# A fused SSD scan and maxout layer: the first four up groups in column halves, and another order of the opening steps

## The chip, the cores and the metric

The kernel runs on one core of one Trainium2 chip. The metric is the time of one execution on the device in microseconds (us), as the median of several runs; lower is better. Five engines work side by side, each through its own instructions in a fixed order: TensorE (PE in the profile; PEld is its loading of weights), VectorE (DVE), ScalarE (ACT), GpSimd (POOL) and SyncE (SP), which issues nearly all transfers. They wait for each other on semaphores.

## The reference, cut to what matters

Two stages follow each other. The first is a state-space scan (Mamba 2) over 4 sequences of 768 tokens with 8 heads; the second is a feed-forward layer whose hidden value is the largest of three products.

```python
# x (4, 8, 768, 32), a (4, 8, 768), B and C (4, 8, 768, 16); chunk c of 32 tokens, state (N x D) per head
cum = np.cumsum(log_a[chunk]);  L = exp(cum[i] - cum[j]) for i >= j, else 0
y[chunk] = ((C @ B.T) * L) @ x + (C @ state) * exp(cum)
state = exp(cum[-1]) * state + sum_j B[j] x[j] * exp(cum[-1] - cum[j])
# then, with y as (3072, 256), w1, w2, w3 (256, 768), w_out (768, 256)
h = np.maximum(np.maximum(y @ w1, y @ w2), y @ w3)
out = h @ w_out
```

## The kernel before, in words

**Blocks.** The kernel scans in blocks of 128 tokens of all four sequences, six blocks in all, so a block gives 512 rows (columns of yT) to the feed-forward layer. It uses max(a, b, c) = b + max(a - b, c - b, 0): the weights w1 and w3 have w2 subtracted, and the part of w2 goes straight to the output through the product w2 @ w_out, the "fold". From block one on both layers' products are done with seven quarter products in place of eight (a Strassen form), which needs sums of weights and of activations beforehand. Block zero does its up products plainly, 512 columns at a time.

**Order.** The tile framework adds the waits, and the program's order is the order of each engine's instructions. For the opening, that is for blocks zero to two of the scan with the up layers of blocks zero and one, this order is written by hand: named steps, and a string ORDER that lists them. Behind it a plan in words (STEADY and LAST) does blocks three to five. The names that matter here, with c for a block, b for a sequence and k or n for a number:

- Loads on SP: `f3` to `f11` fetch a block of weights each (512 KB; 3 to 8 are up weights, 9 to 11 are w_out), `cs` stores the running sums of log a, `lLcb` brings them back spread over 128 rows for sequences b and b+1 (1 MB), `lEc`, `lBc`, `lCc`, `lxc` load the rest, `l3` all of block three.
- Decoding the weights (L193 to L222): `dAk` or `dBk` on ScalarE (two instructions, L200 and L202; in dB the value lies in PSUM), `dVk` on VectorE (three: L208, L211, L213), `dPk` the sum on GpSimd (L220).
- Weights made ready: `vk` subtracts w2 (L693, VectorE), `uk` makes the four sums (L703 to L706, GpSimd); `Tq` and `tq` transpose w2 and copy it, `Fq` multiplies it into the fold, `Fc` copies the fold.
- Scan of block zero: `i`, `j` spread the decays in PSUM (PE), `Xbg` their exponentials (ScalarE, L386), `k02`, `k03` masks for two sequences (GpSimd, L390); `tB`, `tC`, `pB`, `bB`, `pC`, `c00`, `c01` bring B and C into place; `s00`, `s02` the scores (PE, L550) and `w0br` their products with L (VectorE, L558; r is a pair of heads). For two of the pairs `q2`, `q3` copy the scores aside (ScalarE) and `M2`, `M3` multiply on GpSimd (L1034). `y00`, `y02` are the two halves of y, two sequences each (PE, L599), and `Y00`, `Y02` copy them into the halves of yT (ScalarE, L609).
- Up layer of block zero: `Gn` is one group of 512 columns in two matmuls (PE, L658), `Hn` its largest value (ScalarE L1131 for w1, VectorE L1133 for w3). Groups 0, 1 need v0; 2, 3 v1; 4, 5 v2; 6, 7 v3; 8, 9 v4; 10, 11 v5.
- Scan of blocks one and two: `kcb` masks (GpSimd, L429), `xci` four exponentials each (ScalarE, L436), `scb`, `wcbr` as above, `Ec`, `dc`, `oc` the part of the old state, `ycb` the own part of one sequence (PE, L586), `Yc0`, `Yc1` copies (ScalarE, L618), `Sci` sums of halves (VectorE, L633). `Dc`, `Ac`, `Zc`, `z1` carry the state on; `fa`, `fb`, `n`, `N` turn the decays over.
- Up layer of block one: `ek` the first four of seven products (PE, L718), `eak` a copy (ScalarE), `evk` sums (VectorE, L756 to L758), `Kk` the other three products, `Kok`, `Kmk`, `Kpk` what follows (Kp on GpSimd, L846). `Oj` and `Oc` are the down layer of block zero (L961), `Sw`, `So` sums of w_out (GpSimd).

**Buffers.** PSUM has eight banks: four for the scan ("att"), one "ffn", one "sumA", two "sumB"; until block one's layer begins the last three serve the opening too. A step that takes a bank waits for that bank's last reader.

Of the kernel before, what the change touches and what calls it, by code (L numbers as in the profile page):

```python
# [19 lines left out]
def kernel(  # L20
# [24 lines left out]
    P = 128  # L45
# [8 lines left out]
    KD = DM // P  # L54
    NF = DF // P
    BLK = NB * P
# [3 lines left out]
    HB = BLK // 2  # L60
# [18 lines left out]
    def bank(tag, n, shape, name):  # L79
        return ps.tile(shape, FP32, tag=tag, bufs=n, name=name)  # L80
# [10 lines left out]
    def ffn_bank(shape, name):  # L91
        turn["ffn"] += 1
        if shared["ffn"] and turn["ffn"] % 3:
            return bank("sumB", 2, shape, name)
        return bank("ffn", 1, shape, name)
# [4 lines left out]
    for k in range(REP):  # L100
# [5 lines left out]
        out=a_sb,  # L106
# [52 lines left out]
    w_sb = [const.tile([P, KD, DF], FP32, name="w%d" % i) for i in range(3)]  # L159
# [74 lines left out]
    def turn_rows(j, name):  # L234
# [24 lines left out]
        out=mask, in_=mask, pattern=[[1, P]], compare_op=ALU.is_ge, fill=MASKED,  # L259
# [3 lines left out]
        out=pick, in_=ident.rearrange("p (r k) -> p k r", k=BH), op=ALU.add, axis=AX.X)  # L263
    npick = const.tile([P, BH], FP32, name="npick")
    nc.vector.tensor_scalar(
        out=npick, in0=pick, scalar1=-1.0, scalar2=None, op0=ALU.mult)
# [4 lines left out]
        out=hsel, in_=hsel, pattern=[[-N, NH]], compare_op=ALU.is_ge, fill=0.0,  # L271
        base=0, channel_multiplier=1)
    nc.gpsimd.affine_select(
        out=hsel, in_=hsel, pattern=[[N, NH]], compare_op=ALU.is_ge, fill=0.0,
# [3 lines left out]
        out=parity, in_=hsel.rearrange("p (r g) -> p g r", g=2), op=ALU.add, axis=AX.X)  # L278
# [163 lines left out]
    yT = {}  # L442
# [203 lines left out]
    def group(bank, i, f, halves):  # L646

        for r in halves:
            for k in range(KD):
                nc.tensor.matmul(  # L650
                    out=bank[:, r * HB:(r + 1) * HB],
                    lhsT=w_sb[i][:, k, f * P:(f + 1) * P],
                    rhs=yT[0][:, k, r * HB:(r + 1) * HB],
                    start=(k == 0), stop=(k == KD - 1), skip_group_check=True)

    def whole_group(bank, i, f):
        for k in range(KD):
            nc.tensor.matmul(  # L658
                out=bank, lhsT=w_sb[i][:, k, f * P:(f + 1) * P], rhs=yT[0][:, k],
                start=(k == 0), stop=(k == KD - 1))  # L660

# [5 lines left out]
    DIFF = (0, 2)  # L669
# [318 lines left out]
    def step(name, fn, *args):  # L988
        assert name not in steps, name
        steps[name] = lambda: fn(*args)  # L990
# [124 lines left out]

    ups = {}

    def up_products(n):
        q, j = divmod(n, 4)
        i, g = divmod(j, 2)  # L1120
        ups[n] = ffn_bank([P, BLK], "up")
        whole_group(ups[n], DIFF[i], 2 * q + g)

    def up_out(n):
        q, j = divmod(n, 4)
# [8 lines left out]
                out=h_of(0)[:, 2 * q + g], in0=mg, in1=ups[n], op=ALU.max)  # L1134

    for n in range(4 * NQ):
        step("G%d" % n, up_products, n)
        step("H%d" % n, up_out, n)
    step("U", places)
    for k in range(NW):  # L1140
# [61 lines left out]
    for j in range(4 * NB):  # L1202
# [4 lines left out]
    step("So", sums_of_out, "G")  # L1207

    ORDER = """
        i0 lB1 tB j0 pB0 X01 f3 X11 tC pC0 f4 f5 X00 X10 bB0 c00 c01 i2 dA0 cs f6 dV0 lL10 f7 f8 lC1  # L1210
        dP0 s00 w002 f9 lE1 lL12 f10 j2 X21 dA1 X20 X30 k02 n2 w003 dV1 w000 X31 s02 q2 dP1 dB2 N2
        w001 k03 M2 dV2 w020 q3 M3 y00 dP2 dB3 Y00 w021 T0 v0 t0 y02 Y02 dB4 G0 H0 dV3 dP3 v1 G1 dV4
        G2 dB5 dV5 fa n1 dP4 v2 G3 G4 N1 dP5 fb H1 D0 dB6 dB7 dV6 H2 dP6 T1 t1 H4 H3 v3 lx1 pB1 bB1
        dV7 dB8 dV8 k10 k11 G5 G6 H5 dP7 A0 dP8 x10 pC1 n3 v4 x11 x12 lB2 H6 U G7 G8 v5 k12 H7 E1 d1
        x13 f11 c10 c11 k13 N3 H8 G9 H9 s10 dB9 u1 Z0 lC2 T2 t2 w100 x14 dV9 dP9 lL20 dB10 w101 x15
        w102 w103 lE2 G10 G11 x16 dV10 dP10 x17 s12 lL22 F0 w120 H10 w122 lx2 w121 H11 o1 y10 D1 y11
        w123 y12 y13 pB2 Y10 u3 Y11 S10 S11 S12 bB2 S13 F1 u0 alone A1 e0 dB11 dV11 Z1 dP11 u2 ea0
        ev0 K0 Ko0 z1 pC2 e1 D2 E2 F2 ea1 ev1 K1 l3 k21 O0 c20 c21 u5 Ko1 d2 e2 ea2 Km1 k22 Fc O1
        ev2 O2 k20 x20 u4 K2 Ko2 O3 s20 O4 x21 x22 x23 Kp1 O5 O6 e3 w203 k23 ea3 ev3 O7 w201 K3 Oc0
        x24 O8 k30 w200 Ko3 Km3 e4 k31 ea4 ev4 x25 O9 O10 s22 w202 w220 x26 w221 Sw So x27 w223 K4  # L1220
        A2 Ko4 Kp3 o2 x30 x31 e5 ea5 y21 Z2 k32 w222 y23 x32 O11 O12 ev5 y20 K5 Ko5 y22 Y20 O13 Y21
        x33 S20 S21 S22 x34 S23 O14 O15 Oc1 k33
    """

    for word in ORDER.split():
# [120 lines left out]
```

## Time and profile before

| what | value |
|---|---|
| median of 3 runs | 261.57 us (261.48 to 265.43) |
| the profiled execution's own time | 261.05 us |
| its span, first to last instruction | 259.3 us |
| PE busy | 247.7 us (96%) |
| PEld busy | 203.1 us (78%) |
| DVE busy | 173.7 us (67%) |
| ACT busy | 115.0 us (44%) |
| POOL busy | 112.9 us (44%) |
| mean granted clock of TensorE | 0.993 |

The page gives the busy time of each engine, a row of 40 slices of the span (a digit is the busy share in tenths), the granted clock of TensorE in the same slices, and the chain of work that ended last, followed back from the end. The timeline lists one engine's instructions in order of time: start, length, line, operation, tile, shape and count, and in brackets the idle time ahead with what ended it. PE's matmuls are pipelined, and one matmul in float32 is two entries.

### The profile page before, as it was taken

To read this page: it belongs to the slowest core of one execution; us is meant where nothing else is said; L and a number is where in the kernel's file an instruction comes from. 1 tells how busy PE (TensorE), PEld (TensorE's weight loads), DVE (VectorE), ACT (ScalarE), POOL (GpSimd) and SP (SyncE) were. 2 spreads that over 40 slices of the span, in tenths; PEclk is the share of its full clock that TensorE was granted. 3 is DMA by queue.
4 is the path that set the end of the run, shared out by engine and by line. 5 is a ranking of instruction groups with operands and counts; after the bars stand their busy time and mean duration, and the time that the engine had idled before them with its cause. 6 is when DMAs were issued, how large, how long until landed. Compare 5 with 4: busy or idle time off the path is not lost.

```text
span 259.3 us, 5617 instructions
## 1 busy us (share of the span) xinstructions
PE 247.7 (96%) x2145; PEld 203.1 (78%) x2145; DVE 173.7 (67%) x360; ACT 115.0 (44%) x310; POOL 112.9 (44%) x148
## 2 busy tenths in 40 slices
PE   6868999899999999999999999999999999999995
PEld 4435454386888778988899988898889899999994
DVE  5599995977626744777765598566878656645651
ACT  3686889933383846634265525163440211101010
POOL 2078683685999940634072651271240404034000
PEclk9988999999999999999999999999999999999999
DMA  3998969996997620966802945501001001001003
GB/s 106 239 228 286 292 143 260 154 216 159 197 252 125 102 52 1 226 169 83 134 4 53 281 108 97 73 5 40 3 1 40 3 0 43 0 0 43 1 19 105
DMA packets 85371, 28.16 MB, mean 109 GB/s; under 512 B 55392, under 2 KB 82016, under 8 KB 85344
## 3 DMA queue, kind: packets, MB, share of 16 engines
q1 hardware_dynamic: 84752, 27.40, 48.1%
q8 instruction: 17, 0.28, 0.5%
q10 hardware_dynamic: 592, 0.39, 0.5%
q14 instruction: 10, 0.08, 0.1%
HBM read 24.54 MB, written 3.24 MB: 107 GB/s over the span
## 4 chain that ended last, share of the span: by engine, by line
PE 87%; DVE 8%; ACT 2%; issue 1%; DMA 1%; POOL 1%; ACTq 0%; DVEq 0%; POOLq 0%
PE o L887 24%; PE sumB L718 20%; PE sumA L718 15%; PE up L658 7%; PE o L961 6%; PE s L550 4%; PE y L586 4%; DVE L L558 2%; PE y L573 2%; DVE w_u L213 2%; PE fold L823 1%; DVE u L211 1%; DVE u L208 1%; PE spread L368 1%; PE A L513 1%; PE trB L464 1%
## 5 line engine op out<-in xcount | busy, mean ns | idle before, releaser
L436 ACT ACTIVATE L<-L,ncums 128x128 f32<-128x128 f32 x160 | 49.7, 391 | 3.7 <-POOL L L429 3.7
L846 POOL TENSOR_TENSOR rb<-h 128x256 f32<-128x256 f32 x16 | 11.7, 729 | 64.0 <-DVE h L793 63.4
L746 ACT COPY eu<-sumA 128x256 f32<-128x256 f32 x30 | 11.2, 372 | 59.4 <-PE sumA L718 59.4
L718 PE MATMUL sumA<-yT,w 128*128 128x256 f32 x120 | 36.9, 389 | 0.1
L718 PE MATMUL sumB<-yT,rb 128*128 128x256 f32 x120 | 35.9, 381 | 0.4 <-POOL rb L703 0.4
L558 DVE TENSOR_TENSOR L<-s,L 128x512 f32<-128x512 f32 x46 | 29.7, 681 | 7.3 <-PE s L550 4.9
L718 PEld LDWEIGHTS sumB<-yT,rb 128*128 128x128 f32 x120 | 22.6, 190 | 4.1 <-POOL rb L703 0.8
L756 DVE TENSOR_TENSOR eu<-sumA,eu 128x256 f32<-128x256 f32 x30 | 12.7, 423 | 18.2 <-ACT eu L746 18.2
L429 POOL TENSOR_SCALAR_AFFINE_SELECT L<-L 128x1024 f32<-128x1024 f32 x20 | 22.6, 1154 | 4.5 <-DMA L<-cums 4.5
L718 PEld LDWEIGHTS sumA<-yT,w 128*128 128x128 f32 x120 | 19.4, 191 | 4.2 <-DVE rb L780 1.0
L658 PE MATMUL up<-yT,w 128*128 128x512 f32 x48 | 21.7, 597 | 0.7 <-ACT yT L609 0.7
L846 POOL TENSOR_TENSOR w<-h 128x256 f32<-128x256 f32 x12 | 8.7, 729 | 28.0 <-DVE h L793 27.5
L220 POOL TENSOR_TENSOR w<-w_u,w_r 128x512 uint32<-128x512 uint32 x9 | 12.8, 1427 | 15.8 <-DVE w_u L213 13.3
L887 PE MATMUL o<-wo,h 128*128 128x128 f32 x120 | 18.0, 275 | 0.0
L887 PE MATMUL o<-rb,h 128*128 128x128 f32 x120 | 18.0, 275 | 0.0
L718 PE MATMUL sumB<-ys,rb 128*128 128x256 f32 x60 | 17.8, 379 | 0.0
L718 PE MATMUL sumB<-ys,w 128*128 128x256 f32 x60 | 17.8, 379 | 0.0
L718 PE MATMUL sumA<-ys,rb 128*128 128x256 f32 x60 | 17.8, 379 | 0.0
L550 PE MATMUL s<-CT,BT 32*128 32x256 f32 x192 | 15.4, 403 | 1.6 <-ACT L L386 1.1
L658 PEld LDWEIGHTS up<-yT,w 128*128 128x128 f32 x48 | 8.7, 190 | 10.1 <-issue 8.6
L780 DVE TENSOR_TENSOR m<-sumB,eu 128x512 f32<-128x512 f32 x15 | 10.3, 688 | 9.0 <-PE sumB L718 9.0
L887 PEld LDWEIGHTS o<-rb,h 128*128 128x128 f32 x120 | 15.7, 192 | 0.0
(149 smaller groups left out, 518.5 us busy)
## 6 DMA issues: line engine op xcount, KB each, us to landing
L<-cums SPq DMA_DIRECT2D x10, 1024.0 KB, 9.1
rb<-in_moe_w_dram SPq DMA_DIRECT2D x9, 512.0 KB, 6.5
raw_x<-in_x_dram SPq DMA_DIRECT2D x6, 512.0 KB, 6.6
out_dram<-ob SPq DMA_DIRECT2D x10, 256.0 KB, 3.1
rb<-in_moe_w_out_dram SPq DMA_DIRECT2D x3, 512.0 KB, 7.2
E<-cums SPq DMA_DIRECT2D x40, 32.0 KB, 4.0
raw_B<-in_B_dram SPq DMA_DIRECT2D x4, 256.0 KB, 5.8
raw_C<-in_C_dram SPq DMA_DIRECT2D x24, 32.0 KB, 1.9
```

Source lines behind the costliest of these rows:

```text
L220: nc.gpsimd.tensor_tensor(out=dst.bitcast(U32), in0=v.rearrange("p (k f) -> p k f", k=2), in1=r.rearrange("p (k f) -> p k f", k=2), op=ALU ...
L429: nc.gpsimd.affine_select(out=Ls[c][:, b], in_=Ls[c][:, b], pattern=[[0, NH], [1, P]], compare_op=ALU.is_ge, fill=MASKED, base=0, channel_ ...
L436: nc.scalar.activation(L[:, b, h], L[:, b, h], AF.Exp, bias=ncum[c][:, b * NH + h:b * NH + h + 1], scale=1.0)
L550: nc.tensor.matmul(out=s[:, i].rearrange("j g i -> j (g i)"), lhsT=st["BT"][rows, b], rhs=st["CT"][rows, b].rearrange("p g i -> p (g i)"), ...
L558: nc.vector.tensor_tensor(out=M, in0=s, in1=M, op=ALU.mult)
L658: nc.tensor.matmul(out=bank, lhsT=w_sb[i][:, k, f * P:(f + 1) * P], rhs=yT[0][:, k], start=(k == 0), stop=(k == KD - 1))
L718: nc.tensor.matmul(out=bank[:, half], lhsT=left(p, k), rhs=sides[c][p], start=(first and half == 0), stop=True, skip_group_check=True)
L746: nc.scalar.copy(out=eu[:, 0], in_=units[c, k][0][:, 0])
L756: nc.vector.tensor_tensor(out=eu[:, 1], in0=A[:, 1], in1=eu[:, 0], op=ALU.add)
L846: eng.tensor_tensor(out=to, in0=a1, in1=a0, op=ALU.subtract)
L887: nc.tensor.matmul(out=o[SLOT[p]], lhsT=x[:, u * P:(u + 1) * P], rhs=right(p, pair), start=(p in opens and pair == 0), stop=True, skip_gro ...
L961: nc.tensor.matmul(out=o[:, i], lhsT=one, rhs=two, start=(f == 0), stop=(f == NF + KD - 1), skip_group_check=True)
```

## The change

Three things change, and all else stays. First, the groups 0 to 3 of block zero's up layer are done in halves of 256 columns: `gn0` works on the first two sequences' half of yT, `gn1` on the other; both write the same bank. The steps run in the order `g00 Y02 g01 g11 g10 H0 g20 g21 H1 g31 g30`, so one half product is listed ahead of the copy of the second half.

Second, the steps of the opening and of blocks one and two stand in another order. On ScalarE `dA0` moves ahead of `bB0` and `c01`, and X11 behind them; the other exponentials change places. On VectorE `dV1` moves ahead of block zero's first products, `dV2` behind its last, `dV9` ahead of v5, `H10` and `H11` behind block one's sums S10 to S13. On PE `s02` goes ahead of `n2`, `pB1` goes ahead of y02, `G10` ahead of s10, `G11` between s10 and s12, `pC2` between e0 and K0, and F2 behind e2. On SP `lL10` moves behind f7 and f8; all its other transfers keep their order. On GpSimd both masks k02 and k03 go ahead of dP1; dP9, u1, u5 and u3 go ahead of dP10, D1 and u0; z1 goes ahead of dP11; the masks of blocks two and three, Sw, Kp1, So and Kp3 stand in another order, the K and S ones later. `Y20` stands behind x32, x33 and x34.

Third, block two's own part y2b, in three groups with other work between them before, stands as y20, y22, y21, y23 right behind A2 and o2.

```diff
-    def whole_group(bank, i, f):
+    def group(bank, i, f, a, b):
         for k in range(KD):
             nc.tensor.matmul(
-                out=bank, lhsT=w_sb[i][:, k, f * P:(f + 1) * P], rhs=yT[0][:, k],
-                start=(k == 0), stop=(k == KD - 1))
+                out=bank[:, a:b], lhsT=w_sb[i][:, k, f * P:(f + 1) * P],
+                rhs=yT[0][:, k, a:b], start=(k == 0), stop=(k == KD - 1),
+                skip_group_check=True)
...
-    def up_products(n):
+    def up_products(n, a=0, b=BLK):
         q, j = divmod(n, 4)
         i, g = divmod(j, 2)
-        ups[n] = ffn_bank([P, BLK], "up")
-        whole_group(ups[n], DIFF[i], 2 * q + g)
+        if n not in ups:
+            ups[n] = ffn_bank([P, BLK], "up")
+        group(ups[n], DIFF[i], 2 * q + g, a, b)
...
     for n in range(4 * NQ):
-        step("G%d" % n, up_products, n)
+        if n < 4:
+            for r in range(2):
+                step("g%d%d" % (n, r), up_products, n, r * HB, (r + 1) * HB)
+        else:
+            step("G%d" % n, up_products, n)
         step("H%d" % n, up_out, n)
...
     ORDER = """
-        i0 lB1 tB j0 pB0 X01 f3 X11 tC pC0 f4 f5 X00 X10 bB0 c00 c01 i2 dA0 cs f6 dV0 lL10 f7 f8 lC1
-        dP0 s00 w002 f9 lE1 lL12 f10 j2 X21 dA1 X20 X30 k02 n2 w003 dV1 w000 X31 s02 q2 dP1 dB2 N2
-        w001 k03 M2 dV2 w020 q3 M3 y00 dP2 dB3 Y00 w021 T0 v0 t0 y02 Y02 dB4 G0 H0 dV3 dP3 v1 G1 dV4
-        G2 dB5 dV5 fa n1 dP4 v2 G3 G4 N1 dP5 fb H1 D0 dB6 dB7 dV6 H2 dP6 T1 t1 H4 H3 v3 lx1 pB1 bB1
-        dV7 dB8 dV8 k10 k11 G5 G6 H5 dP7 A0 dP8 x10 pC1 n3 v4 x11 x12 lB2 H6 U G7 G8 v5 k12 H7 E1 d1
-        x13 f11 c10 c11 k13 N3 H8 G9 H9 s10 dB9 u1 Z0 lC2 T2 t2 w100 x14 dV9 dP9 lL20 dB10 w101 x15
-        w102 w103 lE2 G10 G11 x16 dV10 dP10 x17 s12 lL22 F0 w120 H10 w122 lx2 w121 H11 o1 y10 D1 y11
-        w123 y12 y13 pB2 Y10 u3 Y11 S10 S11 S12 bB2 S13 F1 u0 alone A1 e0 dB11 dV11 Z1 dP11 u2 ea0
...
+        tB i0 j0 X00 tC X01 X10 pB0 lB1 dA0 f3 f4 f5 pC0 c00 cs f6 f7 bB0 c01 f8 lL10 lC1 X11 i2 s00
+        f9 dV0 dP0 dA1 dV1 j2 X21 s02 X20 k02 w003 n2 X31 lE1 w001 lL12 X30 k03 w002 w000 q3 w020
+        dP1 N2 w021 q2 M2 dB2 y00 Y00 f10 M3 dB3 pB1 dV2 T0 dP2 y02 v0 g00 Y02 g01 g11 g10 dB4 dV3
+        t0 v1 H0 g20 dV4 dP3 dB5 g21 H1 g31 dP4 dV5 dB6 g30 fa n1 fb v2 H2 dP5 N1 D0 dV6 G4 H4 v3
+        bB1 T1 t1 dP6 k10 k11 dB7 dV7 H3 dB8 lx1 dP7 A0 dV8 dP8 v4 k12 x10 n3 lB2 G5 H5 G6 G7 H6 pC1
+        G8 H7 x11 dA9 k13 x12 dV9 dP9 E1 c10 v5 N3 d1 x13 U c11 H8 G9 u1 f11 G10 s10 Z0 w100 w103
+        lC2 w101 H9 dB10 lL20 G11 s12 lE2 w102 dV10 x14 x15 x16 u5 w120 T2 u3 F0 o1 x17 dP10 w121
+        w122 y10 w123 y13 D1 lL22 y11 y12 Y10 alone pB2 u0 F1 A1 Y11 S10 t2 D2 S11 S12 dA11 bB2 S13
+        H11 H10 e0 pC2 ea0 Z1 z1 ev0 lx2 dV11 dP11 K0 Ko0 e1 c20 ea1 O0 ev1 E2 K1 Ko1 u2 Km1 e2 ea2
...
+        w202 w220 Sw O11 O12 x30 K4 Ko4 e5 w223 x31 A2 w222 o2 ea5 y20 Kp1 So w221 y22 y21 k33 y23 ev5
+        x32 K5 Z2 O13 x33 k32 x34 Kp3 O14 O15 Y20 Ko5 Y21 S20 S21 Oc1 S22 S23
     """
```

More of the change, by code (lines that the diff above doesn't have):

```diff
@@ L1215 @@
-        x13 f11 c10 c11 k13 N3 H8 G9 H9 s10 dB9 u1 Z0 lC2 T2 t2 w100 x14 dV9 dP9 lL20 dB10 w101 x15
-        w102 w103 lE2 G10 G11 x16 dV10 dP10 x17 s12 lL22 F0 w120 H10 w122 lx2 w121 H11 o1 y10 D1 y11
-        w123 y12 y13 pB2 Y10 u3 Y11 S10 S11 S12 bB2 S13 F1 u0 alone A1 e0 dB11 dV11 Z1 dP11 u2 ea0
-        ev0 K0 Ko0 z1 pC2 e1 D2 E2 F2 ea1 ev1 K1 l3 k21 O0 c20 c21 u5 Ko1 d2 e2 ea2 Km1 k22 Fc O1
-        ev2 O2 k20 x20 u4 K2 Ko2 O3 s20 O4 x21 x22 x23 Kp1 O5 O6 e3 w203 k23 ea3 ev3 O7 w201 K3 Oc0
@@ L1220 @@
-        x24 O8 k30 w200 Ko3 Km3 e4 k31 ea4 ev4 x25 O9 O10 s22 w202 w220 x26 w221 Sw So x27 w223 K4
-        A2 Ko4 Kp3 o2 x30 x31 e5 ea5 y21 Z2 k32 w222 y23 x32 O11 O12 ev5 y20 K5 Ko5 y22 Y20 O13 Y21
-        x33 S20 S21 S22 x34 S23 O14 O15 Oc1 k33
+        tB i0 j0 X00 tC X01 X10 pB0 lB1 dA0 f3 f4 f5 pC0 c00 cs f6 f7 bB0 c01 f8 lL10 lC1 X11 i2 s00
+        f9 dV0 dP0 dA1 dV1 j2 X21 s02 X20 k02 w003 n2 X31 lE1 w001 lL12 X30 k03 w002 w000 q3 w020
+        dP1 N2 w021 q2 M2 dB2 y00 Y00 f10 M3 dB3 pB1 dV2 T0 dP2 y02 v0 g00 Y02 g01 g11 g10 dB4 dV3
@@ L1223 @@
+        H11 H10 e0 pC2 ea0 Z1 z1 ev0 lx2 dV11 dP11 K0 Ko0 e1 c20 ea1 O0 ev1 E2 K1 Ko1 u2 Km1 e2 ea2
+        F2 Fc k21 k20 d2 c21 k22 ev2 O1 K2 O2 x20 s20 Ko2 e3 O3 l3 k23 x21 x22 x23 w201 w200 ea3
+        w203 O4 k30 O5 ev3 O6 O7 x24 K3 Ko3 x25 Oc0 O8 u4 e4 ea4 x26 x27 k31 Km3 O9 ev4 O10 s22 w202
+        w220 Sw O11 O12 x30 K4 Ko4 e5 w223 x31 A2 w222 o2 ea5 y20 Kp1 So w221 y22 y21 k33 y23 ev5
+        x32 K5 Z2 O13 x33 k32 x34 Kp3 O14 O15 Y20 Ko5 Y21 S20 S21 Oc1 S22 S23
     """
```

## The prediction, made before the changed kernel ran

> **What bounds the kernel now.** I read the page first, then TensorE's timeline, then VectorE's, ScalarE's and GpSimd's over the first 110 us, then single transfers in the DMA view. The page:
>
> ```profile
> span 259.3 us, 5617 instructions
> PE   6868999899999999999999999999999999999995
> PEclk9988999999999999999999999999999999999999
> PE 87%; DVE 8%; ACT 2%; issue 1%; DMA 1%; POOL 1%; ACTq 0%; DVEq 0%; POOLq 0%
> ```
>
> PE is full from slice 4 (26 us) on, and 87% of the chain is PE's. The change removes no multiplication, so it can only win PE's idle time. PE's timeline shows where that is (start, length, [idle before <- releaser]):
>
> ```profile
> 21.98 1.12 PE L599 MATMUL y<-L,raw_x 128*32 128x128 f32 x28 [0.19 <-DVE L L558]
> 23.78 5.42 PE L658 MATMUL up<-yT,w 128*128 128x512 f32 x12 [0.69 <-ACT yT L609]
> 33.51 0.60 PE L464 MATMUL trB<-ident,raw_B 128*128 128x128 f32 x4
> 51.91 1.97 PE L823 MATMUL fold<-wo,rb 128*128 128x256 f32 x8 [1.03 <-DVE w_u L213]
> 59.63 0.70 PE L718 MATMUL sumA<-yT,w 128*128 128x256 f32 x2
> 62.79 0.67 PE L718 MATMUL sumB<-yT,rb 128*128 128x256 f32 x2 [0.41 <-POOL rb L703]
> ```
>
> The up products (G0) start at 23.78, after the second half of yT; F0 waits at 51.9 for VectorE's decode; the first block of e0 and K0 loses time at 62. Behind G0 stand VectorE (score products, then v0) and GpSimd (the products set aside):
>
> ```profile
> 20.65 1.28 DVE L558 TENSOR_TENSOR L<-s,L 128x512 f32<-128x512 f32 x2
> 21.84 0.90 DVE L693 TENSOR_TENSOR w<-w,w 128x512 f32<-128x512 f32 x1
> 38.33 0.68 DVE L693 TENSOR_TENSOR w<-w,w 128x512 f32<-128x512 f32 x1
> ```
> ```profile
> 19.68 2.51 POOL L1034 TENSOR_TENSOR L<-m,L 128x512 f32<-128x512 f32 x2
> 44.66 2.14 POOL L429 TENSOR_SCALAR_AFFINE_SELECT L<-L 128x1024 f32<-128x1024 f32 x2 [4.51 <-DMA L<-cums]
> ```
>
> VectorE has next to no gap from 12 to 42 us, so its order sets what PE may start.
>
> **Part by part.** The profiled execution took 261.05 us (span 259.3 and 1.75 around it), 0.5 below the median of 261.57. Durations are starts of back-to-back instructions in its timelines: ScalarE 0.5 to 0.58 for 512 columns; VectorE 0.60 a score product, 2.06 a decode through PSUM, 1.53 one in SBUF, 0.62 a weight difference; GpSimd 1.28 a decode's sum, 1.07 a mask, 1.25 a product set aside.
>
> *Halves.* Four groups of two matmuls at 0.865 (5.42 for six and a tail) become 16 of 256 columns at 0.43 (L718's from 60.59 to 61.03): 6.9 us both ways. Eight weight loads are added; a load's mean is 190 ns, beside a matmul of 430, so I take 0. Ends: 0, and 8 x 0.19 = 1.5 if they lay bare.
>
> *Opening.* Up to 9.4 all is as before. dA0 (2 x 0.58 on ScalarE; its weights land 4.0 after an issue at 5.42) now stands before bB0 and c01: c01 starts at 11.15, not 10.49. X11 is behind it, so s00's fourth bank comes at 12.35 and s00 ends at 13.1; j2 14.1; four exponentials 14.2 to 16.2; s02 17.1. VectorE: dV0 from 10.5, dV1 from 12.95 to 14.5, four products to 16.9. Then y00, and Y00 by 19.9 (before: 22.55). GpSimd: k02 and k03 to 17.5, dP1 18.7, M2 and M3 21.2 (before 22.19). VectorE: w020, N2, w021 from 17.5 to 19.1 (before 21.93, as dV2 stood ahead), dV2 21.15, v0 21.85. y02's last part takes 1.1 after M2 and M3 began to come: 22.3. So g00 starts at 22.35, 1.4 earlier; v0 is there 0.5 before. g00 covers the copy Y02, which cost 0.69. pB1 (0.44) and T0 fill PE's wait at 19.5 to 21: raw_B lands at 12.11 + 7.4.
>
> *Middle: what is late next.* PE is ahead by 1.4 and 0.44, but VectorE is not. From v0's start to v4's end it took 21.84 to 39.01, 17.17, full. Now v0 starts at 21.15, and dV7 waits some 0.6: its dB7 stands on ScalarE behind H4, bB1 and t1, and H4 waits for G4, G4 for v2 (29.3). v4 ends at 38.9. G8 waits for it and starts at 38.95, 1.55 before the old 40.5, with 0.5 to 0.8 of new idle on PE ahead of it. G8, G9 and G10 (5.2), s10 (44.15 to 45.25), four products to 47.65, dV10 to 49.7, F0 at 49.8 (before 51.91): 2.1 won. dV9, H10 and H11 no longer stand in that stretch; G11, s12 and T2 are done by 49. From F0 to e0 the same instructions took 7.72: e0 at 57.5.
>
> Queues passed on the way. SP: the only new order is lL10 behind f7 and f8. Those two used to wait for the store of cums, since SP stood at 19.9 to 23.7; DMA share fell to 0.15 from 23.5 to 25. They fill that hole, and what follows comes about 1 us earlier (an estimate from that hole): lL10 at 30 to 32, against GpSimd's k10 at 33.5; lL12 at 43.5; f10 at 45.1. GpSimd: k12, k13, dP9, then u1, u5, u3 (1.87 each) now ahead of dP10 (53.9; F1 wants it at 55), D1 (55.0; A1 56.8), u0's third sum (56.4; e0's second product 57.9). ScalarE: dB10 waits for f10, x14 to x17 behind it end at 51.3, w123 at 52.2; y13 comes at 53. Each holds, by 0.8 us at least; gone, the price is one for one. Further on, u4 stands behind k30, whose transfer had landed by 78.1, when that mask ran without a wait: at the latest u4's third sum is ready at 80.6, and e4's second product is due at 81.4. Kp1, So and Kp3 move back to 97 at the latest; their readers, block one's pieces of out, began at 104.3 and will at 100.5.
>
> *e0 and K0.* From 59.63 to 63.73 passed 4.10 for 3.03 of matmuls. pC2 (0.44) now lies between, and H10, H11 (1.2) and Z1 are done on VectorE by 58.2, before ev0's inputs: K0's B part waits 0.1. I take 0.95 won; ends 0.4 and 1.05.
>
> *y of block two.* A change between full and 32-row tiles costs 0.1 each way:
>
> ```profile
> 96.77 0.64 PE L586 MATMUL y<-L,raw_x 128*32 128x128 f32 x16
> 97.34 0.70 PE L718 MATMUL sumA<-yT,w 128*128 128x256 f32 x2
> 97.88 0.59 PE L718 MATMUL sumB<-yT,rb 128*128 128x256 f32 x2
> ```
>
> 97.34 to 97.88 is 0.54, 0.11 over L718's 0.43. Three islands in full tiles become none, A2, o2 and y standing together: six changes, 0.6 won. Y20 now waits on ScalarE for x32 to x34, these for k32, that for Z2: Y20 at 95, S22 at 97.7; block two's first product is due at 98.3. Cover 0.6.
>
> Sum: 2.1 (the 1.4 and 0.44 are in it) + 0.95 + 0.6 = 3.65; 261.05 - 3.65 = **257.4 us**.
>
> **Rivals.** *Half clock over the first groups.* These windows show it:
>
> ```profile
> 14.20:17.60 3.40, 2.27 (x18) 1.31 (x17) 3.33 (x5) 2.51 (x6) 2.02 (x3) 1.00 1.27 195
> 17.60:21.00 3.40, 2.96 (x35) 1.98 (x35) 3.33 (x7) 2.12 (x5) 3.32 (x4) 0.51 0.95 335
> ```
>
> After 3.4 us with much idle, PE had half its clock for 3.4 us, where it cost nothing, as VectorE was late. Now PE waits from 18 to 21 with pB1 and T0 alone; if the next stretch (21.0 to 24.4) is cut, y02's last part costs 1.1 more and the groups 0.5: 259.0. For it: less work there than the 2.96 of before; against it: y00 now falls partly into the first window. [...]
>
> *The halves are hidden anyway.* g00 waits for v0, not only for Y00. If VectorE runs 0.7 later than I walked, g00 goes where whole groups would: 258.0. For it: v0 took 0.90 under GpSimd, not 0.62.
>
> *Slower: lL10 behind f7 and f8.* k10 and k11 stand on GpSimd ahead of dP7; dP7 leads to v4, v4 to G8. Past 34, each us that lL10 is late costs one: landing at 35.5 gives 258.9, and from 38 on the kernel is slower than before (at 39, 262.4). For it: before it landed 6.1 after an issue at 23.7, and two weight blocks of 512 KB now go first; f7 and f8 landed 1.6 apart. Against: the hole in the transfers. 29.8 + 3.2 - 1 to 2 is at most 32.
>
> *Faster.* If dV7's wait and G8's idle go, 1.4 more is won: 256.0.
>
> **How the numbers follow.** Chances: the walk holds 0.50 (its own range 256.3 to 258.3); half clock 0.17; hidden halves 0.12; faster 0.11; lL10 late but not that late 0.07; slower 0.03. The predicted time is the walk's. The range leaves out the slower case, half of the faster one and tails: 255.9 (the faster case) to 260.2 (half clock with 1.2 of the bare loads). 2% of 261.57 is 5.2 us, about what a measurement here can tell from no change. Below 256.3 lie most of the faster case and a tail of the walk: 0.14. Above 266.8 only a part of the last case: 0.02. Within: 0.84.
>
> **What would show it.** PE's first 128x256 up matmul at 22.0 to 22.8 with no wait for yT before the third; idle on PE before G8 released by VectorE's difference; F0 at 49.5 to 50.3; no idle of 0.4 before K0's sumB; one row of y for block two, between rows of A and sumA. Wrong if: PE's clock is halved after 21; GpSimd waits for lL10 past 34; F1 or e0 wait for GpSimd; block two's last Y copies end after 97.

## The result and the profile after

The changed kernel takes 258.1 us (median; 257.95 to 258.78), beside 261.48 to 265.45 for the kernel before on the same chip: ratio 0.987, 95% interval 0.984 to 0.991. Forecast were 257.4 and a range of 255.9 to 260.2. The profiled execution took 258.0 us (span 256.3), 3.05 less than the profiled one before, where the sum said 3.65. One thing has to be known to read the times: those of the kernel before scatter from 261.2 to 266.4 us, and the ratios use only runs within 1.5% of the fastest, so that its medians below (263.1 to 264.75) lie above what a ratio is taken against.

The page of the changed kernel, the lines that were shown of the kernel before:

```profile
span 256.3 us, 5647 instructions
...
PE   6788999999999999999999999999999999999994
...
PEclk9999999999999999999999999999999999999999
...
PE 87%; DVE 5%; ACT 3%; POOL 2%; issue 1%; DMA 1%; ACTq 0%; DVEq 0%
```

VectorE's share of the chain fell from 8% to 5%; the dip in the clock's third and fourth slices is gone. TensorE's timeline (start, length, idle before and its releaser):

```profile
21.21 0.85 PE L599 MATMUL y<-L,raw_x 128*32 128x128 f32 x20 [0.31 <-POOL L L1035]
21.99 7.17 PE L658 MATMUL up<-yT,w 128*128 128x256 f32 x32
...
39.09 5.39 PE L658 MATMUL up<-yT,w 128*128 128x512 f32 x12 [0.23 <-DVE w L694]
...
50.26 1.97 PE L824 MATMUL fold<-wo,rb 128*128 128x256 f32 x8 [0.44 <-DVE w_u L213]
...
57.97 0.70 PE L719 MATMUL sumA<-yT,w 128*128 128x256 f32 x2
...
61.13 0.67 PE L719 MATMUL sumB<-yT,rb 128*128 128x256 f32 x2 [0.29 <-DVE m L759]
```

The first group starts at 21.99 with no wait (23.78 before); G8 waits 0.23 for the weight difference v4, F0 0.44 for the decode dV10, K0's part B 0.29 for VectorE's third sum. The lead over the kernel before is 1.79 at g00, 1.65 at F0 and e0, 2.09 at e1 (62.07 against 64.16), and 3.05 from block two's first product (99.05 against 102.10) to the end. A2, o2 and y of block two now stand in one row; before they stood in four places, A2 with o2 and y in three:

```profile
91.56 0.65 PE L513 MATMUL A<-raw_x,Bd 128*32 128x64 f32 x32
92.15 1.10 PE L573 MATMUL y<-Cd,S 32*64 32x128 f32 x32
93.18 1.96 PE L586 MATMUL y<-L,raw_x 128*32 128x128 f32 x64
95.06 0.70 PE L719 MATMUL sumA<-yT,w 128*128 128x256 f32 x2
```

One part of the change stands in the diff and not in its description: decodes 9 and 11 are `dA` now and were `dB` before, so their value lies in SBUF and takes no bank of PSUM. For decode 9 VectorE took 1.53 us from start to next start (40.05 to 41.58), before 2.06 (45.77 to 47.83). No run has this part by itself.

### The profile page after: what moved, and what is told of

It is laid out like the page before. It is cut to its first block, busy times and chain, and to the rows that moved or that the text cites. A ratio compares the mean times of both kernels' runs of the same rounds, so it can differ in the third digit from the quotient of the medians.

```text
span 256.3 us, 5647 instructions
## 1 busy us (share of the span) xinstructions
PE 246.1 (96%) x2161; PEld 206.2 (80%) x2161; DVE 172.2 (67%) x360; ACT 114.6 (45%) x310; POOL 112.7 (44%) x148
## 4 chain that ended last, share of the span: by engine, by line
PE 87%; DVE 5%; ACT 3%; POOL 2%; issue 1%; DMA 1%; ACTq 0%; DVEq 0%
PE o L888 25%; PE sumB L719 20%; PE sumA L719 16%; PE up L658 6%; PE o L962 5%; PE s L550 4%; PE y L586 4%; PE fold L824 2%; PE y L573 2%; ACT L L386 1%; POOL L L1035 1%; PE spread L380 1%; POOL L L390 1%; DVE u L211 1%; PE spread L368 1%; DVE w_u L213 1%
## 5 line engine op out<-in xcount | busy, mean ns | idle before, releaser
L658 PE MATMUL up<-yT,w 128*128 128x256 f32 (+1 forms) x64 | 21.9, 493 | 0.4 <-DVE w L694 0.2
L847 POOL TENSOR_TENSOR w<-h 128x256 f32<-128x256 f32 x12 | 9.5, 790 | 28.0 <-DVE h L794 27.5
L658 PEld LDWEIGHTS up<-yT,w 128*128 128x128 f32 x64 | 11.7, 189 | 7.9 <-issue 4.9
L550 PEld LDWEIGHTS s<-CT,BT 32*128 32x128 f32 x192 | 10.0, 184 | 7.3 <-ACT L L386 2.2
```

The source lines that it names most:

```text
L550: nc.tensor.matmul(out=s[:, i].rearrange("j g i -> j (g i)"), lhsT=st["BT"][rows, b], rhs=st["CT"][rows, b].rearrange("p g i -> p (g i)"), ...
L658: nc.tensor.matmul(out=bank[:, a:b], lhsT=w_sb[i][:, k, f * P:(f + 1) * P], rhs=yT[0][:, k, a:b], start=(k == 0), stop=(k == KD - 1), skip ...
L847: eng.tensor_tensor(out=to, in0=a1, in1=a0, op=ALU.subtract)
```

## The experiments

An edit that moves steps is shown by the steps of ORDER around it. Starts that are compared come from TensorE's timelines.

### Parts of the change on the kernel before

**The halves alone** (whole groups become halves in their old places):

```
- y02 Y02 dB4 G0 H0 dV3 dP3 v1 G1 dV4 G2 dB5 dV5 fa n1 dP4 v2 G3 G4
+ y02 g00 Y02 g01 dB4 H0 dV3 dP3 v1 g11 g10 dV4 g20 g21 dB5 dV5 fa n1 dP4 v2 g31 g30 G4
```

> The kernel before with the halves alone: each half of the first four groups as soon as its half of yT is there, no other step moved. Theory one (TensorE sets the time from the first groups to s10, and s10 sets F0): the 0.69 us that G0 waited for the copy Y02 are won, s10 starts at 43.3 instead of 44.0, F0 at 51.25 instead of 51.91, and the profiled run takes about 260.4 us. Theory two (VectorE sets the whole stretch up to F0, as the prediction had it): g00 starts earlier, but v4, G8 and F0 stay where they were, 261.0 us. By both the first group's product of 256 columns starts at about 23.1.

Measured 263.03 us (261.25 to 265.15), ratio 1.002 (0.997 to 1.008). Neither theory is borne out by the times, and the profile says why. Its windows (start:end, length, busy us of PE, PEld, DVE, ACT, POOL, then granted clock, DMA share, GB/s):

```profile
19.85:23.26 3.41, 1.32 (x21) 0.62 (x12) 3.14 (x5) 3.32 (x7) 3.33 (x3) 1.00 1.05 375
23.26:26.67 3.41, 3.22 (x33) 2.54 (x32) 3.34 (x7) 1.24 (x3) 2.33 (x3) 0.50 0.64 199
```

TensorE had half its clock from 23.26 to 26.67, as the first groups ran (from 25.31 and not from 23.1; the first four transposes of B, at 8.86, had taken 1.11 us, where the profile before has 0.65). What the halves are worth in this order is left open by this run; half a clock for 3.41 us costs up to 1.7 (an estimate, half of that window), more than the 0.69 that they could win. F0 follows s10 by 7.92 us here (45.99 to 53.91).

**The opening alone** (the steps of the changed kernel up to dV5, the old order behind them):

> The kernel before with the opening of the changed kernel (its steps up to dV5, halves among them), and the old order from there on. Theory one (each part alone wins about what both together win, since VectorE and TensorE cover each other): s10 at about 42.6, VectorE's tenth decode ends at about 50.3, F0 at 50.4 to 50.8, so 1.1 to 1.5 won, 259.6 to 260.0 us. Rival (what pays is the decode dV9 out of the stretch ahead of F0): F0 at 51.5 or later, 260.7 or more. e0 to K0 stays 3.16 long, as before.

Measured 260.24 us (259.89 to 261.07), ratio 0.991 (0.987 to 0.996). s10 came at 42.94 and F0 at

```profile
50.86 1.97 PE L824 MATMUL fold<-wo,rb 128*128 128x256 f32 x8 [1.03 <-DVE w_u L213]
```

1.05 earlier than before, with the same wait of 1.03. F0 follows s10 by 7.92 us here and by 7.91 in the kernel before: in the old order s10, its products, dV9 and dV10 are one chain behind TensorE's groups. The rival is out. Some 0.2 less than expected was won; TensorE waited 0.80 for VectorE ahead of T1. The clock stayed up, and not only here: the mean granted clock is 0.999 or 1.000 in eight of the ten runs and 0.993 in two, while none of the 25 runs of the kernel before beside them is above 0.993.

**VectorE's middle alone** (dV9 with dB9 and dP9 ahead of s10, H10 and H11 behind S13, dV11 with dB11 and dP11 behind ev0):

> The kernel before with VectorE's order changed between v4 and K0 alone: dV9 (with dB9, dP9) ahead of s10, H10 and H11 behind the sums of block one's y, dV11 (with dB11, dP11) behind ev0. Theory one: TensorE was at F0's place at 50.88 and waited 1.03 for dV10; that wait goes and nothing else, F0 at 50.9, 260.0 us. Rival (only an earlier start of the groups pays): F0 stays at 51.9, 261.0 us. If the prediction was right that VectorE's work ahead of ev0 delays K0, K0's part B comes sooner than 3.16 us after e0, and another 0.5 is won; if the chain from e0's sumA through ScalarE's copy and VectorE's three sums has that length by itself, it stays 3.16.

Measured 267.65 us (265.23 to 270.79), ratio 1.013 (1.007 to 1.018). The edit missed its aim. s10 stopped after six products:

```profile
51.41 2.07 PE L550 MATMUL s<-CT,BT 32*128 32x256 f32 x10 [2.76 <-DVE w_u L213]
```

It went on at 51.41, right behind the end of dV9's third instruction (51.36) and ahead of that of Z0 (51.68). That instruction is the last reader of the bank in which dB9 leaves its value, so what s10 missed is most likely this bank; that is read off the order of the times and was not tested. dV9 itself waited 2.96 for ScalarE (dB9). The changed kernel has dA9 in this place, which takes no bank. The granted clock was 0.50 twice, from 23.16 to 29.98 and from 50.47 to 57.29. The question it was made for is not answered by it; the kernels with two and three moves below answer it.

**y of block two alone** (A2, o2, w222 and the four y in one row, the rest behind):

```
- K4 A2 Ko4 Kp3 o2 x30 x31 e5 ea5 y21 Z2 k32 w222 y23 x32 O11 O12 ev5 y20 K5 Ko5 y22 Y20
+ K4 A2 Ko4 Kp3 o2 w222 y20 y21 y22 y23 x30 x31 e5 ea5 Z2 k32 x32 O11 O12 ev5 K5 Ko5 Y20
```

> The kernel before with y of block two in one row behind A2 and o2, no other step moved but the product w222 that it needs and the later steps that stand behind. Three places fewer where TensorE leaves its full tiles. By the prediction's price (0.1 us a change, 0.2 a place) 0.6 won, 260.4 us; by what the changed kernel's trace gave (0.95 between e1 and block two) 0.32 a place, 0.95 won, 260.1 us. If the copies behind y make block two's first product wait, less.

Measured 264.48 us (260.82 to 265.41), ratio 1.0 (0.993 to 1.007). The profiled execution had a granted clock of 0.50 from 23.87 to 30.69, so the whole time says nothing; the stretch does. Against the profile before, its e1 and all that follows up to 77 us come 4.46 later, and block two's products from 113 us on 3.59 later: 0.87 won in between, 0.29 for each of three places. That is nearer to 0.95 than to 0.6.

### The clock

**Idle TensorE filled with useless work, in the kernel before.** T0's transposes are done four times:

```
- for g in range(2):
+ for g in [g for _ in range(4 if q == 0 else 1) for g in range(2)]:
```

> The kernel before with T0's four transposes done four times over into the same bank (1.3 us of work for TensorE that gives nothing new), in the place where TensorE waits for VectorE ahead of y02; nothing else is changed. Two profiles of variants of the kernel before had TensorE at half clock for 3.4 and 6.8 us from 23.3 and 23.9 us on, in the first groups, after a wait of 2.1 us at 20.7; each 3.4 us so cut costs 1.7. Clock theory: with the wait filled the clock stays up in the first groups, and the median falls to between 261.3 and 262.3, with hardly a run above 262.5, though there is more work. Rival (the scatter of 261.2 to 265.6 in the kernel before has another cause): the same scatter and median, or 0.3 more for the added work, 263.1 to 263.4.

Measured 262.55 us (262.23 to 264.21), beside 264.75 (261.46 to 266.18) for the kernel before in the same series; ratio 0.996 (0.992 to 1.000). TensorE's timeline, and a window as above:

```profile
20.08 1.97 PE L809 MATMUL w2T_tp<-ident,w 128*128 128x128 f32 x16
22.77 0.41 PE L599 MATMUL y<-L,raw_x 128*32 128x128 f32 x4 [0.73 <-DVE L L558]
```
```profile
19.57:22.98 3.41, 2.68 (x42) 2.18 (x31) 2.95 (x5) 3.41 (x7) 3.33 (x4) 1.00 1.04 365
```

With the wait filled the clock stayed up in this execution (1.00 from 22.98 to 26.39 too), and a kernel with 1.3 us more work had a median 2.2 us lower. The ratio, whose interval reaches 1, shows no difference by itself. The mean granted clocks of the runs say more: four of the twelve are at 1.000, four at 0.993, four at 0.986 to 0.987; of the 23 of the kernel before none is above 0.993, and nine are at 0.985 or lower. So the useless work makes cuts fewer and does not end them. That speaks for the clock theory, but half of the kernel's runs lie above 262.5, where hardly one was expected. One reason can be seen in the profiled execution, in which the first four transposes of B took 1.11 us, where the profile before has 0.65, and the groups started 1.34 later (25.12).

**T0 and pB1 out of the wait, in the changed kernel** (behind g31 and g30):

> The changed kernel with T0 (and t0) and pB1 moved from TensorE's wait ahead of y02 to behind g31 and g30; the order of all else is as in the changed kernel. By the work alone: 0.9 us of TensorE's work now stands among the groups, of which the waits ahead of G5 and G8 (0.5) take in about half, 258.2 to 258.6 us, all runs close together. Clock theory: TensorE now waits 2 us or more with nothing to do, as in the kernel before; in some runs the clock is halved over the first groups, and these lie 1.7 or 3.4 higher, 260 to 262 us.

Measured 260.06 us (259.86 to 261.34), ratio 0.987 (0.981 to 0.992). Both expectations missed. The clock stayed up (mean granted clock 0.998 to 1.000 in all six runs), and the loss was 1.90 at e0 instead of 0.2 to 0.6: 0.87 for the two steps, and a wait that was not seen to come:

```profile
31.09 0.24 PE L323 MATMUL from_j_tp<-ident,passing 32*128 32x32 f32 x1 [0.80 <-ACT passing L315]
```

Both steps filled time that TensorE had for nothing; behind the groups they cost their full length and delay what stands behind them.

**Whole groups in the changed kernel** (v0 Y02 G0 G1, G2 and G3 in the places of the first halves):

> The changed kernel with the first four groups whole again, in the places of their first halves but behind Y02. Theory one (the halves win what they let start earlier, because TensorE's progress sets G4, H4, dB7 and so v4): G0 at 22.75 instead of 21.99, v4, G8 and F0 0.6 to 0.77 later, 258.6 to 258.8 us. Theory two (VectorE's decodes set v4 and G8 whatever TensorE does): G8 and F0 unmoved, 258.0 us.

Measured 259.38 us (258.71 to 262.51), ratio 0.985 (0.978 to 0.992). Its lowest time is 0.76 above the changed kernel's in the first series and 0.60 above that of the series below, which is theory one; the three series were not all run on one chip. Its profile (262.51 us) fell in an execution with a second price:

```profile
20.55:23.96 3.41, 1.88 (x35) 1.22 (x34) 3.31 (x6) 2.69 (x6) 3.15 (x3) 1.00 1.06 397
23.96:27.37 3.41, 3.41 (x5) 1.35 (x5) 3.31 (x6) 1.34 (x4) 1.58 (x1) 0.50 1.04 391
```

Without halves TensorE waits 0.68 more for Y02; here it was busy for 1.88 of 3.41 us and had a granted clock of 0.50 over the groups. The other five runs took 258.71 to 259.67.

**The changed kernel again:**

> The changed kernel itself once more, for its times beside the other kernels on one chip. If its opening always keeps TensorE's clock up in the first groups, its runs lie within 1 us of 258.0. If the clock's stretches can still fall so that the first groups are cut, as in the profile of the whole groups (half clock from 23.96 to 27.38), some runs lie 1.5 to 3 us higher.

Measured 258.38 us (258.11 to 258.99), beside 261.55 to 266.43 for the kernel before; ratio 0.984 (0.980 to 0.989). All are within 1 us of 258.0. Nine of the ten runs of both series have a mean granted clock of 1.000; one has 0.993, as much as one cut of 3.41 us, and with 258.11 it is the lowest of its series, so that cut fell where it cost nothing that the time shows. The spread has another source: in this profile (258.55) dV3 waited 0.35 for ScalarE's dB4, and F0 came at 50.70.

### The rival that ended slower

**lL10 one place later** (behind lC1):

> The changed kernel with lL10 one place later on SP's queue, behind lC1, which waits for a free buffer until 27.6. lL10 is issued 3.4 us later and lands at 36.3 instead of 32.9. By the prediction's rival (each us past 34 costs one, by k10, dP7, v4, G8): 2.3 us, 260.3. By the changed kernel's trace: k10 and k11 end at 38.45, dP7 at 39.7, v4 starts at 39.7 instead of 38.25, G8 1.45 later, 259.4 us. If the transfers are hidden as they stand: 258.0.

Measured 260.35 us (258.88 to 262.26), ratio 0.992 (0.985 to 0.999). The median lies between two groups: three runs of 258.88 to 259.07 with a mean granted clock of 0.998 to 1.000, and three of 261.62 to 262.26 with 0.986 to 0.993, so that its nearness to the rival's 260.3 says nothing. The profiled execution took 259.07. Its groups start 1.08 later than in the changed kernel (23.07); why was not shown. GpSimd's mask k10, and G8 on TensorE:

```profile
34.95 2.14 POOL L429 TENSOR_SCALAR_AFFINE_SELECT L<-L 128x1024 f32<-128x1024 f32 x2 [0.16 <-DMA L<-cums]
```
```profile
40.14 5.39 PE L658 MATMUL up<-yT,w 128*128 128x512 f32 x12 [0.23 <-DVE w L694]
```

v4 (39.31) and G8 are 1.06 and 1.05 later, as late as the groups and no later; k10, 1.25 later, cost nothing. SP's issue of lL10 ended 4.4 us later (28.64 against 24.21), but the transfer landed at 34.9, only 2.0 later. The first two expectations fall. "Hidden" holds for this execution, whose late groups gave k10 as much more room; what the move costs when the groups start early is not shown. The rival's point (34) was too early by the changed kernel's own trace too: dP7 ended at 37.1 and v4 starts at 38.25, so 1.1 us of slack lay between, and by that k10 may start until 34.8.

### What was left to win

**Three moves at the three waits that are left** (the kernel's order, around each):

```
- c10 v5 N3 d1 x13 U c11 H8 G9 u1 f11 G10 s10 Z0 w100
+ c10 c11 v5 N3 d1 x13 U H8 G9 u1 f11 s10 G10 w100      (Z0 behind v4)
- y13 D1 lL22 y11 y12 Y10 alone pB2 u0 F1 A1
+ y13 D1 A1 lL22 y11 y12 Y10 alone u0 F1
- dA11 bB2 S13 H11 H10 e0 pC2 ea0
+ dA11 S13 H11 H10 e0 pC2 pB2 bB2 ea0
```

> The changed kernel with three moves, each at a wait that its trace still shows: (1) s10 one group earlier, ahead of G10, with c11 and Z0 moved up: F0 no longer waits for dV10, 0.44; (2) A1 directly behind y13, one place fewer where TensorE leaves its full tiles: 0.32 by what the y of block two gave, 0.2 by the prediction's price; (3) pB2 from ahead of F1 to behind pC2, into the hole ahead of K0's part B: 0.49 if K0's part B is set by the chain from e0's sumA alone (3.16 us after e0 whatever else moves), nothing if VectorE's other work sets it. All three: 256.7 to 256.9 us; by the prediction's reading of K0 and of the places 257.3.

Measured 260.89 us (260.45 to 263.05): some 2.6 slower than the changed kernel, and yet the first move does what it should.

```profile
49.32 1.89 PE L824 MATMUL fold<-wo,rb 128*128 128x256 f32 x8
...
55.12 0.65 PE L513 MATMUL A<-raw_x,Bd 128*32 128x64 f32 x32 [1.87 <-POOL Bd L503]
...
62.91 0.70 PE L719 MATMUL sumA<-yT,w 128*128 128x256 f32 x2 [1.41 <-DVE eu L757]
```

F0 starts 0.94 earlier without a wait. The other two each set a new wait, for the same kind of reason: A1 waits for D1, which stands on GpSimd behind three sets of weight sums, and holds up half of y; and bB2 holds up ScalarE until pB2 is done, with ea0, the copy of e0's sum, behind it.

**Two moves** (s10 as above, pB2 behind pC2, but bB2 behind ea0; A1 and D1 as in the changed kernel):

> The changed kernel with two moves: s10 (with c11 and Z0 ahead of it) one group earlier, and pB2 from ahead of F1 to behind pC2, its copy bB2 now behind ea0. The kernel with three moves had shown F0 at 49.32 with no wait, and then two new waits: A1 for D1, 1.9 us, and K0 for ea0's copy, 1.4, since ScalarE stood at bB2. Theory: those two waits came of A1's place and of bB2 ahead of ea0; without them e0 starts at 56.5, K0's part B follows 3.16 after it, at 59.7, and the profiled run takes 256.5 to 256.7 us. Rival (the hole ahead of K0 can't be filled, since what fills it delays the chain behind e0): K0's part B later than 60.1, 257.0 us.

Measured 257.5 us (257.45 to 257.69), ratio 0.981 (0.976 to 0.986).

```profile
54.87 1.99 PE L824 MATMUL fold<-wo,rb 128*128 128x256 f32 x8 [0.50 <-POOL wo L220]
...
57.38 0.70 PE L719 MATMUL sumA<-yT,w 128*128 128x256 f32 x2
...
60.54 0.67 PE L719 MATMUL sumB<-yT,rb 128*128 128x256 f32 x2
```

K0's part B follows e0 by 3.16 with no wait left: the hole can be filled. The time is 0.8 above the theory's. F1's wait of 0.50 for dP10 is the larger part of it: lL12 landed at 44.8, not 43.6, and GpSimd's masks k12 and k13 with all behind them came 1.2 later. Why it landed later is not settled.

**Three moves again** (D1 behind N3, A1 behind y12, u3 behind u0):

> The kernel with two moves and a third: A1 directly behind the last step of block one's y (with alone ahead of it), D1 on GpSimd ahead of u1, and u3 behind u0, so that A1 finds its operand ready. One place fewer where TensorE leaves its full tiles. 0.3 us less than with two moves (0.29 to 0.32 a place by the y of block two), 256.2 to 256.4 us; by the prediction's price 0.2. If GpSimd's sums now come too late (D1 stands ahead of u1, u5, dP10), F1 or e0 waits and the gain is lost.

Measured 257.03 us (256.37 to 257.34), ratio 0.979 (0.974 to 0.983), the lowest of all kernels here; of the expected 256.2 to 256.4 only its lowest run is. In its profile the first four transposes of B took 1.12 us (0.66 in the changed kernel's) and the groups started 0.90 later (22.89); nevertheless it ended 0.8 sooner.

```profile
57.16 0.59 PE L719 MATMUL sumA<-yT,w 128*128 128x256 f32 x2
...
60.21 0.67 PE L719 MATMUL sumB<-yT,rb 128*128 128x256 f32 x2
```

From y's L586 to e0's second product TensorE took 4.60 us, in the changed kernel 5.31, of which 0.49 are pB2: A1's place was worth 0.22. GpSimd's sums came in time.

## Why the prediction was right, and where it was not

The time was in the range and in the walk's own (256.3 to 258.3); the order of the waits was read rightly from VectorE's timeline. The sum by its steps, in us won by the profiled executions:

| step | forecast | measured |
|---|---|---|
| g00's start | 22.35 | 21.99 |
| v4's end, G8's start | 38.9, 38.95 | 38.93, 39.09 |
| won at F0 | 2.1 | 1.65 |
| won from e0 to e1 (K0's block) | 0.95 | 0.44 |
| won from e1 to block two (y) | 0.6 | 0.95 |
| sum | 3.65 | 3.04 (the times: 3.05) |

Two terms came out 0.45 and 0.51 too large and one 0.35 too small; that they cancel in part, so that the sum is off by only 0.6, is luck.

*Opening.* Right, g00 0.36 earlier still. v0 ended at 21.84 (forecast 21.85), as VectorE's row shows:

```profile
21.16 0.68 DVE L694 TENSOR_TENSOR w<-w,w 128x512 f32<-128x512 f32 x1
...
38.25 0.68 DVE L694 TENSOR_TENSOR w<-w,w 128x512 f32<-128x512 f32 x1
```

y02's last part took 0.8 after the set-aside products began to come, not 1.1. v4 ran in the place that was walked, though dV7 waited 0.91, not 0.6; G8's idle was 0.23.

*F0.* 0.46 short. G8 came 0.14 and s10 0.25 later than walked, s10's products ended 0.3 later (47.97), and dV10 with F0 behind it the rest. The mechanism, F0 set by the decode behind s10's products, held: with s10 one group earlier F0 came at 49.32 without a wait.

*K0.* The step that failed: "H10, H11 (1.2) and Z1 are done on VectorE by 58.2, before ev0's inputs: K0's B part waits 0.1". They were, and it did not matter. From e0's first product to K0's part B passed 3.16 us in the kernel before (59.63 to 62.79), 3.16 in the changed one (57.97 to 61.13) and 3.16 with two moves (57.38 to 60.54): it is one chain, e0's sumA, ScalarE's copy, VectorE's three sums. With three moves it is 3.05 (57.16 to 60.21), as e0's first product is 0.1 shorter; from its second product it is 2.62 or 2.63 in all four. In the changed kernel VectorE stood idle for 1.0 us just before, waiting for that copy:

```profile
59.54 0.42 DVE L757 TENSOR_TENSOR eu<-sumA,eu 128x256 f32<-128x256 f32 x1 [1.01 <-ACT eu L747]
```

The old trace showed VectorE busy right up to ev0's first sum at 61.20, but ScalarE's copy ended at 61.17 too, so that two ends met there:

```profile
60.80 0.37 ACT L746 COPY eu<-sumA 128x256 f32<-128x256 f32 x1 [1.52 <-PE sumA L718]
60.80 0.41 DVE L524 TENSOR_TENSOR S<-A,parity 128x256 f32<-128x256 f32 x1
61.20 0.42 DVE L756 TENSOR_TENSOR eu<-sumA,eu 128x256 f32<-128x256 f32 x1
62.22 0.42 DVE L758 TENSOR_TENSOR m<-sumB,v 128x256 f32<-128x256 f32 x1
```

The prediction took the engine for the bound and not the chain. Its row for K0's part B names GpSimd (L703) as what ended the wait; the third sum ended at 62.64, 0.15 ahead of the product, as in the changed kernel (60.98 and 61.13). Only pC2's 0.43 in the hole was won, near the forecast's lower end of 0.4.

*y of block two.* Right mechanism, wrong size: a place cost 0.29 to 0.32, not 0.2. The rows of before would have given it: 16 products of y took 0.57 from start to next start, 32 took 1.01, so each island has 0.13 of its own beside the 0.1 at either side that was counted. One sign of being wrong did come: block two's last Y copies ended at 98.04, past 97 (Y20 was walked to 95), and S22 at 98.87. The first product started at 99.05 without a wait, so it cost nothing.

*The halves, and the rivals.* "Hidden anyway" is out: whole groups in the same order cost 0.6 to 0.8 by the lowest times. The price of the bare weight loads was rightly taken at about 0: the 32 entries of the halves took 7.1 us, where the sum had 6.9. The slower rival was given a point from which it decides (34) that is 0.8 too early. lL10 itself landed at 32.9 and not at 30 to 32, 9.1 us behind its issue where 6.1 had passed before; k10 started at 33.70 without a wait for it. The faster one (1.4 for dV7's wait and G8's idle) did not come.

*Half clock.* The prediction put this rival on the changed kernel, because the one profile that it had showed the cut where it did no harm ("it cost nothing, as VectorE was late"). The runs showed it the other way round. In profiles of three variants of the kernel before, the cut fell on the first groups (from 23.16, 23.26 and 23.87 us on); two of these have the opening of the kernel before, whose own profile shows it from 17.64 to 21.05, so its place varies. All 59 runs of the kernel before in three series have a mean granted clock of 0.974 to 0.993, so each had a cut somewhere: at 0.993 they took 261.2 to 262.0 us, at 0.974 to 0.981 264.7 to 266.4, and at 0.987 from 261.6 to 266.2, so that the mean clock alone does not set the time. Of the changed kernel's ten runs nine are at 1.000, and with its opening alone on the kernel before eight of ten are at 0.999 or 1.000. The new opening thus does away with most cuts, a gain that was not forecast. By the medians of one series the change wins 4.8 (263.15 to 258.38) and not 3.05, but the ratio's interval (0.980 to 0.989) is too wide to tell the two apart. That the one profile before had a cut that cost nothing, so that the sum started from a low 261.05, is luck for the forecast time. How the times of the kernel before divide among a late opening, a short cut and a long one was not settled, for want of a profile of each.

## What to carry to other kernels

Ask of every wait whether an engine's queue ends last or a chain of dependent steps that passes through it: two traces with the same distance (3.16 us here) between first and last link, whatever the queue holds, mark a chain, and a chain's hole is filled with other work, not shortened by clearing the queue. A moved step is paid for on the queue of whoever consumes it (bB2 ahead of ea0, D1 behind three sums, dV9 behind a late dB9), so walk its producer and its consumer too. A kernel whose times scatter should be profiled more than once before one profile's clock is taken as its own: work that merely fills an early wait can be worth more than its place in the sum (T0 and pB1 took 0.87 us; with both out of the wait e0 came 1.90 later).

## What the runs showed of the hardware

*Where the clock fell.* In five profiles the granted clock of TensorE was 0.50 for 3.41 or 6.82 us at a time. TensorE's busy time in the 3.41 us ahead:

| kernel | busy in the 3.41 us ahead, us | clock at 0.50, us |
|---|---|---|
| before | 2.28 | 17.64 to 21.05 |
| the halves alone | 1.32 | 23.26 to 26.67 |
| VectorE's middle alone | 1.32 | 23.16 to 29.98 |
| VectorE's middle alone, later | 1.59 | 50.47 to 57.29 |
| y of block two alone | 1.14 | 23.87 to 30.69 |
| whole groups in the changed kernel | 1.88 | 23.96 to 27.37 |

The changed kernel had TensorE busy throughout in about the stretch where the kernel before had 2.28 us of work (14.23 to 17.64):

```profile
15.28:18.69 3.41, 3.41 (x51) 2.30 (x51) 3.41 (x7) 2.20 (x5) 3.39 (x4) 1.00 0.93 97
```

The clock was 1.00 in the next 3.41 us, and also behind 2.60 us of work in the changed kernel (18.69 to 22.10), 2.54 with lL10 one place later (20.57 to 23.98), 2.68 with T0 done four times (19.57 to 22.98), and 2.66 in the second kernel with three moves:

```profile
20.21:23.62 3.41, 2.66 (x40) 1.93 (x39) 3.31 (x6) 2.58 (x6) 3.18 (x3) 1.00 1.06 380
```

Little work did not always bring a cut: the first kernel with three moves was busy for 1.54 us from 52.95 to 56.36 and had 1.00 from there to 59.77; the changed kernel without T0 and pB1 was busy for 2.01 from 18.69 to 22.10, and the mean granted clock of that execution is 0.999. What decides where a cut falls, and how much work is enough there, was not shown.

*How fast the first transposes ran.* The first four transposes of B took 0.65 or 0.66 us in the profiles of the kernel before, the changed kernel, the opening alone, the changed kernel without T0 and pB1 and the first kernel with three moves, and 1.11 or 1.12 in those of the halves alone, VectorE's middle alone, y of block two alone, T0 done four times, whole groups and the second kernel with three moves.

*A place of 32-row tiles among full ones* cost 0.29 us for y in the kernel with y of block two alone (0.87 for three places) and 0.32 in the changed kernel (0.95 for three), and 0.22 for A1 (32 products; the second kernel with three moves against the changed kernel), the change of tile at either end and the place's own start together.
